# Attention woven between the matmuls of the MLP in one written-out order

## The chip, the cores and the metric

The kernel runs on 1 core of one Trainium2 chip. The core has five engines with queues of their own: PE (TensorE, matmuls; its weight loads are shown as PEld), DVE (VectorE), ACT (ScalarE), POOL (GpSimd) and SP (SyncE, which here only issues DMAs). SBUF is the working memory, PSUM the memory that PE writes its results to. The metric is the device time of one execution in microseconds (us), the median of several runs.

## The reference, cut to what matters

Two stages. The first is a linear attention with a decaying state, for 4 batches, 8 heads, 768 positions and head size 48:

```python
for t in range(S):
    cur = np.einsum('bhd,bhe->bhde', u[None] * kt, vt)
    y[:, :, t] = np.einsum('bhd,bhde->bhe', rt, state + cur)
    state = wt[:, :, :, None] * state + np.einsum('bhd,bhe->bhde', kt, vt)
```

Its output, as 3072 tokens of 8 x 48 = 384 features, goes through an MLP with 2048 hidden features:

```python
h = x @ w_in            # [3072, 384] @ [384, 2048]
r = np.maximum(h, 0.0)
g = s * (r * r) + b
return (g @ w_out).astype(np.float32)   # [3072, 2048] @ [2048, 384]
```

All inputs and the output are fp32.

## The kernel before, in words

Attention works on chunks of 128 positions: 4 batches x 6 chunks = 24 chunks, one batch after the other, each with all 8 heads. Per chunk, four loads (`rt`, `kt`, `vt`, issued by POOL and cast to bf16 on the way, L100 to L106; `wt`, fp32, issued by SP, L109). ACT takes the logarithm of w (`logw`, L114), PE forms its running sums by two triangular matmuls (`cums_i`, `cums_e`, L119, L126) and the sums of a whole chunk by eight one-column matmuls (L131). ACT takes the exponentials (`RA` L141, `KAi` L144, `lam` L153), DVE multiplies r and k by them (`PRD`, L165, L173), PE transposes the products per pair of heads (`trps`, L202), ACT copies them out (`RTKT`, L211), PE forms the scores (`mt_ps`, L217), DVE masks them (`mt_sb`, L227), PE multiplies by v and by the state (`y_ps`, L238, L255). The state goes on by `delta_ps` (L269), an addition on DVE (L291) and a product on POOL (L297); the odd heads' states are moved to partitions 64 to 111 by a DMA on SP (L309). POOL and DVE form the diagonal term (L183, L185, L188, L190), DVE adds it (`x_sb`, L321), PE transposes the result (L330) and ACT copies it to `xT` (L338), which holds the input of the MLP for all 3072 tokens.

The MLP is written behind the attention. The sum of w_out over its rows, times b, comes first (L347 to L360). Then there are six tiles of 512 tokens. For each, 16 groups of 3 matmuls give 128 hidden features by 512 tokens (`h_ps`, L367), ACT takes the relu (`rh`, L375), DVE squares it (`gT`, L376); after those, four groups of 16 matmuls give 128 tokens by 384 features (`o_ps`, L389), DVE scales and adds (`o_sb`, L399), SP stores (L408).

The framework's scheduler sets the order of each engine's instructions, by the order in the text and by when inputs are ready. It also loads ACT's function table anew where logarithm and exponential follow each other (21 + 13 + 6 + 2 loads in the profile).

Of the kernel before, what the change touches and what calls it, by code (L numbers as in the profile page):

```python
# [16 lines left out]
def kernel(  # L18
# [16 lines left out]
    L = 128  # L35
    NCH = S // L
    HD = H * D
    d_model, d_ff = moe_w_in.shape
    n_tok = out.shape[0]
    KT = d_model // 128  # L40
    FT = d_ff // 128
    TOKCH = 512
    NTC = n_tok // TOKCH
# [4 lines left out]
    make_identity(nc, identity)  # L48

    tri_strict = const.tile([128, 128], BF16, name="tri_strict", tag="tri_strict")  # L50
    make_upper_triangular(nc, tri_strict, val=1.0, diag=False)
    tri_incl = const.tile([128, 128], BF16, name="tri_incl", tag="tri_incl")
    make_upper_triangular(nc, tri_incl, val=1.0, diag=True)

    ones_col = const.tile([128, 1], BF16, name="ones_col", tag="ones_col")
    nc.gpsimd.memset(ones_col, 1.0)
    ones_row = const.tile([1, 128], BF16, name="ones_row", tag="ones_row")
    nc.gpsimd.memset(ones_row, 1.0)

    u_bc = const.tile([128, H, D], BF16, name="u_bc", tag="u_bc")  # L60
    nc.gpsimd.dma_start(out=u_bc, in_=u.partition_broadcast(128))

    s_bc = const.tile([128, 1], FP32, name="s_bc", tag="s_bc")
    nc.sync.dma_start(out=s_bc, in_=moe_s.partition_broadcast(128))
    b_sc = const.tile([1, 1], FP32, name="b_sc", tag="b_sc")
    nc.sync.dma_start(out=b_sc, in_=moe_b.partition_broadcast(1))

    w_in_sb = const.tile([128, KT, d_ff], BF16, name="w_in_sb", tag="w_in_sb")
    nc.gpsimd.dma_start(
        out=w_in_sb, in_=moe_w_in.rearrange("(kt p) f -> p kt f", p=128)  # L70
    )
    w_out_sb = const.tile([128, FT, d_model], BF16, name="w_out_sb", tag="w_out_sb")
    nc.gpsimd.dma_start(
        out=w_out_sb, in_=moe_w_out.rearrange("(ft p) n -> p ft n", p=128)
    )

    xT = const.tile([128, KT, n_tok], BF16, name="xT", tag="xT")
    bconst = const.tile([128, d_model], FP32, name="bconst", tag="bconst")

    with (  # L80
        tc.tile_pool(name="ain", bufs=1) as ain,
        tc.tile_pool(name="aprep", bufs=1) as aprep,
        tc.tile_pool(name="atrans", bufs=1) as atrans,
        tc.tile_pool(name="astate", bufs=1) as astate,
        tc.tile_pool(name="apsum", bufs=1, space=bass.MemoryType.PSUM) as apsum,
    ):
        state0 = None
        state_pk = None
        for bb in range(B):
            for cc in range(NCH):  # L90
                t0 = cc * L
                tok0 = bb * S + t0
                is_first = cc == 0
                is_last = cc == NCH - 1

                rt = ain.tile([128, H, D], BF16, name="rt", tag="rt", bufs=3)
                kt_ = ain.tile([128, H, D], BF16, name="kt", tag="kt", bufs=3)
                vt = ain.tile([128, H, D], BF16, name="vt", tag="vt", bufs=3)
# [340 lines left out]
```

## Time and profile before

| what | value |
|---|---|
| median of 3 runs | 344.73 us (343.74 to 346.08) |
| span of the profiled execution, first to last instruction | 342.3 us |
| the profiled execution's own time | not listed; the three runs shown lie 1.4 to 3.8 us above the span |
| PE busy | 235.2 us, 69% of the span |
| DVE, ACT, POOL busy | 186.5, 181.9, 152.7 us |
| DMA | 20.44 MB, 110233 packets, 104578 of them under 512 bytes |

The busy times are sums over the whole span, and the span has two stages with different limits: attention until about 209 us and the MLP behind it. A busy share says little without the stage that it belongs to. In the chain of waits the MLP's two matmul lines hold 18.2% of the span each, and no other line holds over 5%.

### The profile page before, as it was taken

To read this page: it belongs to the slowest core of one execution; us is meant where nothing else is said; L and a number is where in the kernel's file an instruction comes from. 1 tells how busy PE (TensorE), PEld (TensorE's weight loads), DVE (VectorE), ACT (ScalarE), POOL (GpSimd) and SP (SyncE) were. 2 spreads that over 40 slices of the span, in tenths; PEclk is the share of its full clock that TensorE was granted. 3 is DMA by queue.
4 is the path that set the end of the run, shared out by engine and by line. 5 is a ranking of instruction groups with operands and counts; after the bars stand their busy time and mean duration, and the time that the engine had idled before them with its cause. 6 is when DMAs were issued, how large, how long until landed. Compare 5 with 4: busy or idle time off the path is not lost.

```text
span 342.3 us, 5002 instructions
## 1 busy us (share of the span) xinstructions
PE 235.2 (69%) x1865; PEld 142.0 (41%) x1865; DVE 186.5 (54%) x260; ACT 181.9 (53%) x280; POOL 152.7 (45%) x199
## 2 busy tenths in 40 slices
PE   1112646565644567555566747999999999999995
PEld 0001434344432344443445523455554545546453
DVE  0001658775457448675468531855829367393761
ACT  4064665856638966679762420924609155190740
POOL 9102999999998779887793510000000000000000
PEclk9999999999999999999999999999999999999999
DMA  7999899999997978979492400001010110201101
GB/s 113 201 182 131 55 64 68 116 63 75 71 69 61 94 60 65 72 59 82 28 52 13 25 6 0 0 25 69 2 69 24 48 46 2 93 0 48 46 23 69
DMA packets 110233, 20.44 MB, mean 60 GB/s; under 512 B 104578, under 2 KB 109826, under 8 KB 110210
## 3 DMA queue, kind: packets, MB, share of 16 engines
q0 software_dynamic: 77488, 10.33, 45.5%
q1 hardware_dynamic: 32722, 9.81, 13.3%
q8 instruction: 14, 0.23, 0.3%
q14 instruction: 9, 0.07, 0.1%
HBM read 25.36 MB, written 4.72 MB: 88 GB/s over the span
## 4 chain that ended last, share of the span: by engine, by line
PE 46%; ACT 11%; POOL 7%; issue 6%; DVE 5%; DMA 5%; DVEq 0%; POOLq 0%; ACTq 0%
PE o_ps L389 18%; PE h_ps L367 18%; DMA vt<-in_v_dram 5%; ACT L114 3%; DVE mt_sb L227 2%; PE trps L202 2%; ACT RTKT L211 2%; PE mt_ps L217 2%; POOL state L297 2%; ACT logw L114 2%; PE colsum_ps L347 1%; PE y_ps L238 1%; DVE PRD L173 1%; POOL rk L183 1%; POOL rt L100 1%
## 5 line engine op out<-in xcount | busy, mean ns | idle before, releaser
L375 ACT ACTIVATE rh<-h_ps 128x512 bf16<-128x512 f32 x96 | 57.3, 597 | 56.9 <-DVE o_sb L399 52.2
L376 DVE SCALAR_TENSOR_TENSOR gT<-rh 128x512 bf16<-128x512 bf16 x96 | 62.5, 692 | 10.8 <-ACT rh L375 10.8
L389 PE MATMUL o_ps<-w_out_sb,gT 128*128 128x384 bf16 x384 | 63.4, 326 | 0.0
L367 PE MATMUL h_ps<-xT,w_in_sb 128*128 128x512 bf16 x288 | 63.3, 379 | 0.0
L389 PEld LDWEIGHTS <-gT 128*128 128x128 bf16 x384 | 37.6, 98 | 25.5
L367 PEld LDWEIGHTS <-w_in_sb 128*128 128x128 bf16 x288 | 28.0, 98 | 33.5 <-issue 0.5
L126 PE MATMUL cums_e<-logw,tri_strict 128*128 128x384 bf16 x24 | 11.6, 482 | 44.0 <-ACT logw L114 25.8
L202 PE MATMUL trps<-identity,PRD 128*112 128x128 bf16 x192 | 29.1, 312 | 15.5 <-DVE PRD L165 8.8
L399 DVE SCALAR_TENSOR_TENSOR o_sb<-o_ps,s_bc,bconst 128x384 f32<-128x384 f32 x24 | 14.8, 617 | 43.4 <-PE o_ps L389 43.4
L165 DVE SCALAR_TENSOR_TENSOR PRD<-rt,RA 128x384 bf16<-128x384 bf16 x24 | 18.4, 766 | 34.7 <-DMA rt<-in_r_dram 31.8
L183 POOL TENSOR_TENSOR rk<-rt,kt 128x384 bf16<-128x384 bf16 x24 | 24.2, 1007 | 23.0 <-DMA kt<-in_k_dram 22.8
L211 ACT COPY RTKT<-trps 112x1024 bf16<-112x1024 bf16 x24 | 24.1, 1006 | 17.6 <-PE y_ps L255 13.9
L202 PEld LDWEIGHTS <-PRD 128*112 128x112 bf16 x192 | 24.7, 204 | 20.9 <-issue 16.0
L114 ACT ACT_TABLE_LOAD x21 | 26.9, 1283 | 11.5 <-DMA wt<-in_w_dram 9.5
L227 DVE TENSOR_TENSOR mt_sb<-mt_ps,tri_strict 128x1024 bf16<-128x1024 f32 x24 | 29.2, 1215 | 6.5 <-PE mt_ps L217 6.5
L173 DVE SCALAR_TENSOR_TENSOR PRD<-kt,KAi 128x384 bf16<-128x384 bf16 x24 | 30.3, 1261 | 3.1 <-DMA kt<-in_k_dram 2.5
L188 DVE TENSOR_REDUCE cdiag<-rku 128x8 bf16<-128x384 bf16 x24 | 13.2, 549 | 32.6 <-POOL ydiag L190 20.6
L106 POOL DMA_DIRECT2D vt<-in_v_dram x24 | 22.4, 933 | 14.0 <-PE y_ps L255 10.8
L185 POOL TENSOR_TENSOR rku<-rk,u_bc 128x384 bf16<-128x384 bf16 x24 | 24.5, 1022 | 1.1 <-DVE cdiag L188 0.7
L144 ACT ACTIVATE KAi<-cums_i 128x384 bf16<-128x384 f32 x24 | 11.8, 490 | 24.1 <-PE cums_i L131 15.8
L100 POOL DMA_DIRECT2D rt<-in_r_dram x24 | 22.1, 922 | 0.0
L103 POOL DMA_DIRECT2D kt<-in_k_dram x24 | 22.0, 918 | 0.0
(50 smaller groups left out, 280.6 us busy)
## 6 DMA issues: line engine op xcount, KB each, us to landing
wt<-in_w_dram SPq DMA_DIRECT2D x24, 192.0 KB, 3.3
out_dram<-o_sb SPq DMA_DIRECT2D x24, 192.0 KB, 1.9
rt<-in_r_dram POOLq DMA_DIRECT2D x24, 96.0 KB, 3.4
kt<-in_k_dram POOLq DMA_DIRECT2D x24, 96.0 KB, 3.5
vt<-in_v_dram POOLq DMA_DIRECT2D x24, 96.0 KB, 3.3
w_in_sb<-in_moe_w_in_dram POOLq DMA_DIRECT2D x1, 1536.0 KB, 13.9
w_out_sb<-in_moe_w_out_dram POOLq DMA_DIRECT2D x1, 1536.0 KB, 23.8
state_pk<-state SPq DMA_DIRECT2D x20, 18.0 KB, 2.0
```

What stands on the lines that cost most here:

```text
L100: nc.gpsimd.dma_start(out=rt, in_=r[bb, :, t0 : t0 + L, :].transpose([1, 0, 2]))
L114: nc.scalar.activation(out=logw, in_=wt, func=AF.Ln)
L173: nc.vector.scalar_tensor_tensor(out=PRD[:, 1, :, :, 0:48], in0=kt_v, scalar=1.0, in1=KAi_v, op0=ALU.bypass, op1=ALU.mult,)
L183: nc.gpsimd.tensor_tensor(out=rk, in0=rt, in1=kt_, op=ALU.mult)
L185: nc.gpsimd.tensor_tensor(out=rku, in0=rk, in1=u_bc, op=ALU.mult)
L202: nc.tensor.matmul(trps[0:112, slot, :], lhsT=src[:, 0:112], rhs=identity, is_transpose=True, start=(slot == 0), stop=(slot == 7),)
L211: nc.any.tensor_copy(out=RTKT[0:112], in_=trps[0:112])
L227: nc.vector.tensor_tensor(out=mt_sb, in0=mt_ps, in1=tri_strict.unsqueeze(1).to_broadcast([128, H, 128]), op=ALU.mult,)
L367: nc.tensor.matmul(h_ps, lhsT=w_in_sb[:, kt, ft * 128 : (ft + 1) * 128], rhs=xT[:, kt, T * TOKCH : (T + 1) * TOKCH], start=(kt == 0), stop ...
L375: nc.scalar.activation(out=rh, in_=h_ps, func=AF.Relu)
L376: nc.vector.scalar_tensor_tensor(out=gT[:, ft, :], in0=rh, scalar=1.0, in1=rh, op0=ALU.bypass, op1=ALU.mult,)
L389: nc.tensor.matmul(o_ps, lhsT=gT[:, ft, tt * 128 : (tt + 1) * 128], rhs=w_out_sb[:, ft, :], start=(ft == 0), stop=(ft == FT - 1),)
```

## The change

The whole kernel is one written-out order. Every step is a function that issues its instructions, and a list of keys sets when each is called; the framework's scheduler is switched off (`manual_schedule`), so each engine runs its instructions in the order of the keys.

Chunks are numbered with the batch as the fast index (chunk n is position chunk n // 4 of batch n % 4), and an MLP tile is one position chunk of all four batches, 512 tokens. The first four chunks stand 2 keys apart ahead of key 0, all others 4 keys apart from key 0 on. A key holds one group of 3 `h_ps` matmuls (`g1`) with its relu and square, and from tile 1 on one quarter of an `o_ps` group (`g2`, 4 matmuls) of the tile before.

Other edits: all loads are fp32 on SP's queue; the weights come in 8 pieces of 0.8 MB through a staging buffer and POOL casts them (`cast_in`, `cast_out`); POOL also casts v (`vb`). Head pairs are padded from 96 to 128 rows, with zeros set once, so the state of a pair is one block and the DMA of the odd heads falls away; one exponential over 768 columns stands in for two, one product over 768 columns for two; the transposed products are copied out in two halves, on DVE and on ACT; one function table holds logarithm and exponential and is loaded once. The square is a plain `tensor_tensor`. PSUM: one two-bank buffer that `cums` and `mt_ps` share (tag "A"), two banks for `trps`, `d_ps`, `y_ps`, `xt_ps` (tag "B"), three for `h_ps`, one for `o_ps`.

```diff
+    ctx.enter_context(tc.manual_schedule())
+    nc.scalar.preload_act_table_set("natural_log_exp_and_others")
...
+    def load(n):
...
+        for src, dst in ((w, c["w"]), (r, c["rk"][:, 0]), (k, c["rk"][:, 1]), (v, c["v"])):
+            nc.sync.dma_start(out=dst, in_=src[bb, :, t0 : t0 + L, :].transpose([1, 0, 2]))
...
+    def pool1(n):
+        nc.gpsimd.tensor_tensor(out=rkp, in0=..., in1=..., op=ALU.mult)
+        nc.gpsimd.tensor_tensor(out=rku..., in0=rkp, in1=u_bc, op=ALU.mult)
+        nc.gpsimd.tensor_copy(out=vb, in_=c["v"])
...
+    def pool2(n):
+        nc.gpsimd.tensor_tensor(out=yd, in0=c["v"], in1=c["cd"]..., op=ALU.mult)
...
+    def cum(n):
+        ps = psA.tile([128, 2, 512], FP32, name="cums", tag="A")
...
+    def expo(n):
+        nc.scalar.activation(out=E, in_=ps[:, :, 0:HD], func=AF.Exp)
+            nc.scalar.activation(out=lam, in_=ps[:, 0, HD : HD + HP], func=AF.Exp)
...
+    def mult(n):
+        nc.vector.tensor_tensor(out=prd..., in0=c["rk"]..., in1=c["E"]..., op=ALU.mult)
...
+    def tevac(n):
+        nc.vector.tensor_copy(out=RT, in_=c["trps"][:, 0:HP, :])
+        nc.scalar.copy(out=KT_, in_=c["trps"][:, HP : 2 * HP, :])
...
+    def mt(n):
+        ps = psA.tile([128, 2, HP, 128], FP32, name="mt_ps", tag="A")
...
+    def square(T, ft):
+        nc.vector.tensor_tensor(out=gT[T][:, ft, :], in0=rh, in1=rh, op=ALU.mult)
...
+    def base(n):
+        return -24 + 2 * n if n < B else 4 * (n - B)
+    for n in range(N):
+        q = base(n)
+        at(q + 0.00, ln, n)
+        at(q + 0.01, pool1, n)
+        at(q + 1.20, cum, n)
+        at(q + 2.00, expo, n)
+        at(q + 2.01, cdiag, n)
+        at(q + 3.00, mult, n)
+        at(q + 3.01, lam2, n)
+        at(q + 3.02, pool2, n)
+        at(q + 4.20, trans, n)
+        at(q + 5.00, tevac, n)
+        at(q + 6.20, mt, n)
+        at(q + 7.00, mask, n)
+        at(q + 8.10, dmm, n)
+        at(q + 8.30, supd, n)
+        at(q + 8.20, ymm, n)
+        at(q + 9.00, yevac, n)
+        at(q + 10.20, xtr, n)
+        at(q + 11.00, xevac, n)
+    def g1key(T, i):
+        return i if T == 0 else 24 + 16 * (T - 1) + i
+    def g2key(T, i):
+        return 17.5 + 1.4 * i if T == 0 else g1key(T, 15) + 2 + i
+    for T in range(NT):
+        for ft in range(FT):
+            q = g1key(T, ft)
+            at(q + 0.40, g1, T, ft)
+            at(q + 0.45, relu, T, ft)
+            at(q + 1.10, square, T, ft)
...
+    order = [(load, 1), (load_win, 0), (load, 2), (load_win, 1), (load, 3)]
+    order += [(load_win, 2), (load_win, 3), (load_wout, 0), (load_wout, 1)]
+    order += [(load, 4), (load_wout, 2), (load_wout, 3), (load, 5), (load, 6)]
...
+    for i in range(NPIECE):
+        at(-10 + i, cast_in, i)
+        at(1.05 + 3 * i, cast_out, i)
```

Three places in the order. In the rows a number behind a name tells one buffer from another.

PE, a chunk's scores. Before, in the attention stage, all that PE has between two score groups is attention:

```order
L217 MATMUL mt_ps_1120<-RTKT_1118 128x128
...
L202 MATMUL trps_1286<-identity_58,PRD_1274 112x128
...
L119 MATMUL cums_i_1448<-logw_1446,tri_incl_68 128x384
...
L269 MATMUL delta_ps_1317<-vt_1248,PRD_1274 48x48
...
L238 MATMUL y_ps_1131<-vt_1071,mt_sb_1129 128x48
...
L330 MATMUL xt_ps_1165<-identity_58,x_sb_1163 128x128
```

Now, from `cums` of one chunk to `mt_ps` of the chunk before it (`h_ps` and `o_ps` are the MLP's):

```order
L169 MATMUL cums_1648<-logw2_104,tri_strict_86 128x384
...
L413 MATMUL h_ps_1655<-xT_1193,w_in0_94 128x512
...
L446 MATMUL o_ps_1668<-w_out0_98,gT_1125 128x384
...
L364 MATMUL xt_ps_1680<-identity_85,x_sb_1641 128x128
...
L255 MATMUL mt_ps_1684<-RT_1643,KTr_1644 128x128
```

One group of `h_ps`, one of `o_ps` and three transposes stand between the two, and `cums` and `mt_ps` take turns in one PSUM buffer.

ACT at the same place. Before:

```order
L211 COPY RTKT<-trps 112x1024
L144 ACTIVATE KAi<-cums_i 128x384
L114 ACT_TABLE_LOAD
L114 ACTIVATE logw<-wt 128x384
L338 COPY xT<-xt_ps 128x3x128
L141 ACT_TABLE_LOAD
L141 ACTIVATE RA<-cums_e 128x384
```

Now, four keys:

```order
L426 ACTIVATE rh_1639<-h_ps_1635 128x512
L245 COPY KTr_1644<-trps_1621 128x512
L426 ACTIVATE rh_1659<-h_ps_1655 128x512
L191 ACTIVATE E_1673<-cums_1648 128x768
L195 ACTIVATE lam_1675<-cums_1648 128x4
L426 ACTIVATE rh_1697<-h_ps_1693 128x512
L379 COPY xT_1703<-xt_ps_1680 128x3x128
L426 ACTIVATE rh_1717<-h_ps_1713 128x512
L127 ACTIVATE logw0_102<-wt_1286 128x8x48
```

The table loads are gone, four relus stand between the attention's steps, and the exponential `E` of a chunk stands behind a relu whose `h_ps` comes behind that chunk's `cums` on PE.

POOL ahead of the first MLP group. Before, POOL's rows are attention steps and load issues:

```order
L183 TENSOR_TENSOR rk<-rt,kt 128x384
L185 TENSOR_TENSOR rku<-rk,u_bc 128x384
L100 DMA rt<-in_r_dram 128x8x48
L297 TENSOR_TENSOR state_1157<-stmp,lam 48x384
L106 DMA vt<-in_v_dram 128x8x48
L190 TENSOR_TENSOR ydiag<-vt,cdiag 128x384
```

Now, with the last of the first four chunks (`yd_380` is chunk 3's):

```order
L156 TENSOR_TENSOR yd_320<-vt_149,cd_285 128x384
L215 TENSOR_TENSOR l2_378<-lam_331,par_89 128x8
L156 TENSOR_TENSOR yd_380<-vt_158,cd_333 128x384
L528 CAST w_in0_94<-wi_st_145 128x1536
L528 CAST w_in1_95<-wi_st_154 128x1536
L528 CAST w_in2_96<-wi_st_163 128x1536
L528 CAST w_in3_97<-wi_st_165 128x1536
L132 TENSOR_TENSOR rkp_497<-rkt_172 128x384
```

POOL issues no loads any more, and four casts of 1536 columns stand back to back.

## Rows read from the trace of the kernel before

**Rows 1.** The page: length of the span, number of instructions.

```profile
span 342.3 us, 5002 instructions
```

**Rows 2.** Busy time by stretch: PE, PEld, DVE, ACT, POOL, then clock, DMA, GB/s.

```profile
30.00:209.00 179.00, 101.69 (x1146) 72.77 (x1147) 109.06 (x140) 111.53 (x165) 143.01 (x177) 1.00 0.86 60
```

**Rows 3.** Chain of waits in order of time, the end: start us, us, what.

```profile
224.56 10.40 PE o_ps L389 x64
234.96 10.36 PE h_ps L367 x48
...
338.80 0.62 DVE o_sb L399
```

**Rows 4.** Timeline, weight loads of the first MLP matmuls (384 columns): start, length, instruction.

```profile
211.89 0.13 PEld L347 LDWEIGHTS <-ones_col 128*1 128x1 bf16 x1 [0.19 <-issue]
212.21 0.13 PEld L347 LDWEIGHTS <-ones_col 128*1 128x1 bf16 x1 [0.19 <-issue]
```

**Rows 5.** Groups by line and form, ACT: busy us, mean ns | idle us before.

```profile
L375 ACT ACTIVATE rh<-h_ps 128x512 bf16<-128x512 f32 x96 | 57.3, 597 | 56.9 <-DVE o_sb L399 52.2
L144 ACT ACTIVATE KAi<-cums_i 128x384 bf16<-128x384 f32 x24 | 11.8, 490 | 24.1 <-PE cums_i L131 15.8 <-PE cums_i L119 4.1 <-DVE PRD L173 4.1
```

**Rows 6.** The same view, DVE.

```profile
L376 DVE SCALAR_TENSOR_TENSOR gT<-rh 128x512 bf16<-128x512 bf16 x96 | 62.5, 692 | 10.8 <-ACT rh L375 10.8
L173 DVE SCALAR_TENSOR_TENSOR PRD<-kt,KAi 128x384 bf16<-128x384 bf16 x24 | 30.3, 1261 | 3.1 <-DMA kt<-in_k_dram 2.5 <-ACT KAi L144 0.4
L227 DVE TENSOR_TENSOR mt_sb<-mt_ps,tri_strict 128x1024 bf16<-128x1024 f32 x24 | 29.2, 1215 | 6.5 <-PE mt_ps L217 6.5
L165 DVE SCALAR_TENSOR_TENSOR PRD<-rt,RA 128x384 bf16<-128x384 bf16 x24 | 18.4, 766 | 34.7 <-DMA rt<-in_r_dram 31.8 <-PE delta_ps L269 2.8
L399 DVE SCALAR_TENSOR_TENSOR o_sb<-o_ps,s_bc,bconst 128x384 f32<-128x384 f32 x24 | 14.8, 617 | 43.4 <-PE o_ps L389 43.4
L321 DVE TENSOR_TENSOR x_sb<-y_ps,ydiag 128x384 bf16<-128x384 f32 x24 | 13.3, 556 | 14.4 <-PE y_ps L255 13.2 <-PE y_ps L238 1.0
L188 DVE TENSOR_REDUCE cdiag<-rku 128x8 bf16<-128x384 bf16 x24 | 13.2, 549 | 32.6 <-POOL ydiag L190 20.6 <-POOL rku L185 12.0
L291 DVE TENSOR_TENSOR stmp<-delta_ps,state 48x384 bf16<-48x384 f32 x16 | 8.7, 543 | 7.4 <-POOL state L297 6.4 <-PE delta_ps L269 0.9
```

**Rows 7.** Tile rt: duration ns, least/median/most.

```profile
L165 DVE SCALAR_TENSOR_TENSOR PRD<-rt,RA x24: 537/594/1372, 29.8 to 187.4; 128x384 bf16<-128x384 bf16 x24
```

**Rows 8.** Groups by line and form, POOL.

```profile
L297 POOL TENSOR_TENSOR state<-stmp,lam 48x384 bf16<-48x384 bf16 x16 | 13.4, 836 | 5.3 <-issue 3.2 <-PE y_ps L255 1.9
L160 POOL MEMSET PRD<- 128x128 bf16 x24 | 5.1, 214 | 3.2 <-PE delta_ps L269 2.5 <-PE trps L202 0.6
L423 POOL MEMSET const-float32-1.0<- 128x1 f32 x1 | 0.1, 98 | 0.0
```

**Rows 9.** Timeline, DVE, 54 to 59 us.

```profile
54.12 3.53 DVE L173 SCALAR_TENSOR_TENSOR PRD<-kt,KAi 128x384 bf16<-128x384 bf16 x1 [0.95 <-DMA kt<-in_k_dram]
57.57 1.21 DVE L227 TENSOR_TENSOR mt_sb<-mt_ps,tri_strict 128x1024 bf16<-128x1024 f32 x1
```

**Rows 10.** Timeline, POOL, the same stretch.

```profile
54.65 0.93 POOL L183 TENSOR_TENSOR rk<-rt,kt 128x384 bf16<-128x384 bf16 x1
55.53 0.83 POOL L190 TENSOR_TENSOR ydiag<-vt,cdiag 128x384 bf16<-128x384 bf16 x1
56.31 0.91 POOL L185 TENSOR_TENSOR rku<-rk,u_bc 128x384 bf16<-128x384 bf16 x1
```

**Rows 11.** SP's DMA queue, 120 to 200 us: packets, MB, share of 16 engines.

```profile
q1 hardware_dynamic: 7288, 1.17, 8.8%
```

**Rows 12.** The same queue, 215 to 342.3 us (stores of 1536-byte rows).

```profile
q1 hardware_dynamic: 3456, 4.72, 10.4%
```

**Rows 13.** The page: load of w by SP, KB each, us to landing.

```profile
wt<-in_w_dram SPq DMA_DIRECT2D x24, 192.0 KB, 3.3
```

More of the change, by code (lines that the diff above doesn't have):

```diff
@@ new lines @@
+    ones = const.tile([128, 128], BF16, name="ones", tag="ones")
+    par = const.tile([128, 2], FP32, name="par", tag="par")
+    u_bc = const.tile([128, HD], FP32, name="u_bc", tag="u_bc")
+    s_bc = const.tile([128, 1], FP32, name="s_bc", tag="s_bc")
+    b_bc = const.tile([128, 1], FP32, name="b_bc", tag="b_bc")
+    bconst = const.tile([128, d_model], FP32, name="bconst", tag="bconst")
+    w_in_sb = [
+        const.tile([128, KT, PW], BF16, name=f"w_in{i}", tag=f"w_in{i}")
+        for i in range(NPIECE)
+    ]
@@ new lines @@
+    w_out_sb = [
+        const.tile([128, FPP, d_model], BF16, name=f"w_out{i}", tag=f"w_out{i}")
+        for i in range(NPIECE)
+    ]
+    NLW = 3
+    logws = [
+        const.tile([128, H, 64], BF16, name=f"logw{i}", tag=f"logw{i}")
+        for i in range(NLW)
+    ]
+    NPR = 3
+    prds = [
+        const.tile([128, 2, H, 64], BF16, name=f"prd{i}", tag=f"prd{i}")
+        for i in range(NPR)
+    ]
+    cb = [dict() for _ in range(N)]
+    xT = [None] * NT
+    gT = [None] * NT
+    states = [None] * B
@@ new lines, in xtr, with xevac @@
+    def xtr(n):
+        c = cb[n]
+        ps = psB.tile([128, KT, 128], BF16, name="xt_ps", tag="B")
+        for i in range(KT):
+            nc.tensor.matmul(
+                ps[:, i, :],
+                lhsT=c["x"][:, i * 128 : (i + 1) * 128],
+                rhs=identity,
+                is_transpose=True,
+                start=(i == 0),
+                stop=(i == KT - 1),
+            )
+        c["xt_ps"] = ps
+    def xevac(n):
+        c = cb[n]
+        cc, bb = coords(n)
+        if bb == 0:
+            xT[cc] = mlp.tile([128, KT, TOK], BF16, name="xT", tag="xT", bufs=2)
+        nc.scalar.copy(
+            out=xT[cc][:, :, bb * L : (bb + 1) * L], in_=c["xt_ps"]
+        )
@@ new lines, in cast_in, with cast_out @@
+    def cast_in(i):
+        nc.gpsimd.tensor_copy(out=w_in_sb[i], in_=w_in_st[i])
+    def cast_out(i):
+        nc.gpsimd.tensor_copy(out=w_out_sb[i], in_=w_out_st[i])
+    load(0)
+    nc.sync.dma_start(
+        out=u_bc, in_=u.rearrange("h d -> (h d)").partition_broadcast(128)
+    )
+    nc.vector.memset(logws[0], 0.0)
+    make_upper_triangular(nc, tri_strict, val=1.0, diag=False)
+    make_upper_triangular(nc, ntri_incl, val=-1.0, diag=True)
+    make_identity(nc, identity)
+    for i in range(1, NLW):
+        nc.vector.memset(logws[i], 0.0)
@@ L412, with small @@
+    for i in range(NPIECE):
+        at(-10 + i, cast_in, i)
+        at(1.05 + 3 * i, cast_out, i)
+    at(17.3, colsum)
+    def small():
+        nc.sync.dma_start(out=s_bc, in_=moe_s.partition_broadcast(128))
+        nc.sync.dma_start(out=b_bc, in_=moe_b.partition_broadcast(128))
+    at(6.03, small)
+    for n in range(8, N):
+        at(base(n) - 14.5, load, n)
+    ev.sort(key=lambda e: (e[0], e[1]))
+    for _, _, fn, a in ev:
+        fn(*a)
 _INS = ['r', 'k', 'v', 'w', 'u', 'moe_w_in', 'moe_w_out', 'moe_s', 'moe_b']
```

673 lines of the change are left out of this document (340 added, 333 removed).

## The prediction

> **What bounds the kernel now.** I read the page first, then the busy time by stretch, the end of the chain of waits, the groups by line, and at last single stretches of the timeline. The span is 342.3 us [rows 1]. From 30 to 209 us, the attention, PE is busy for 101.7 of 179 us and POOL for 143.0 [rows 2]; no engine is full, and the engines wait for one another along chunk after chunk. Behind that the chain has nothing but matmuls: 64 of `o_ps` in 10.40 us and 48 of `h_ps` in 10.36 us [rows 3], alternating six times, so 124.6 us in which PE is full and the others are not. A group of 4 `o_ps` or 3 `h_ps` matmuls thus takes 0.65 us. The first matmuls behind the attention are started by weight loads 0.32 us apart [rows 4]: 384 columns in 0.32 us are 1.2 GHz, though the granted clock in the rows reads 1.00; the 0.1625 us of `o_ps` are 2.4 GHz. So the attention's matmuls run at the lower level, the MLP's at the upper. The profile's own execution is not listed; I sum against the span and add 344.73 - 342.3 = 2.4 us to stand by the median.
>
> **The change, part by part.** It lays the attention (some 180 us in which PE has room) beside the MLP. The kernel then falls into four pieces.
>
> *Start, until the first `h_ps`: 46 us.* It needs chunks 0 to 3 complete. SP issues 16 loads for them, with two pieces of w_in and `u_bc` between. A load is 1024 packets of 192 bytes; SP's queue moved 7288 small packets in 8.8% of 80 us [rows 11], so 1.0 us a load on 16 engines; at most it is the 3.3 us from issue to landing [rows 13], if they ran one by one. They are queued up to eight deep, so I take 1.0. A 0.79 MB piece is a sixth of the stores' 4.72 MB, which took 10.4% of 127.3 us [rows 12]: 2.2 us. So 1 + 16 x 1.0 + 2 x 2.2 + 0.5, and 2.3 for the last landing: 24 us. Then POOL does four products of 0.84 us [rows 8] and a cast of v, 4 us, and stands before its four weight casts. No row has a cast on POOL. Lower bound: the memset's (214 - 98)/127 = 0.91 ns a column [rows 8], 1.5 us for 1536; upper bound: the two-input product's 836/384 = 2.2 ns [rows 8], 3.3 us. One input lies between, nearer to the memset: I take 2.0, so POOL is through at 36 us.
>
> Chunk 3's product on DVE meets this. In the profile a DVE product that takes 0.537 us alone [rows 7] was asked for at 54.12 us and lasted 3.53 us [rows 9]: POOL's three products ran back to back from 54.65 until 57.22 [rows 10], and DVE came in behind the last. I expect the same behind the four casts: the product ends at 37 us, and transposes, copies, scores, mask (1.2 us [rows 6]), y, addition and copy take 7 to 9 us at the lower clock. First `h_ps` at 46 us, 37 if the casts held nobody up, 56 if they took 3.3 us and the loads half as long again.
>
> *Woven stretch, one chunk in four keys: 19 periods of 8.4 us, 160 us.* PE per period: 4 groups of `h_ps` and 4 of `o_ps`, 5.2 us [rows 3]; attention 101.7/24 = 4.2 us a chunk at 1.2 GHz [rows 2], half of it at 2.4 GHz, 2.1 us. Sum 7.3. Added is a wait: `cums` and `mt_ps` share a PSUM buffer, so a chunk's scores wait for the next chunk's exponential. ACT takes a relu first (0.6 us [rows 5]), which waits for the `h_ps` behind those `cums`, then 768 columns, 0.49 + 384 x (0.597 - 0.490)/128 = 0.81 us [rows 5], and the small exponential, 0.2. PE has one `o_ps` group and three transposes meanwhile, 0.8 us, so about 0.9 us of stall with everything in PE's queue behind it, the MLP too: 8.2 us.
>
> DVE per period: mask 1.2, two additions 1.1, sum for the diagonal 0.55, output 0.62 [rows 6]; the 768-column product, 0.54 + 384 x (0.692 - 0.537)/128 = 1.0 [rows 6, 7]; a copy of 512 columns from PSUM, 0.6 by interpolation from the addition's 384; four squares. The square was 0.692 us [rows 6] as another operation on the same data; that is the upper bound, half of it, at twice the rate, the lower. I take 0.5, since the fixed part stays. Sum 7.1; successive instructions overlap by 0.08 us (57.65 against 57.57 [rows 9]), 12 of them give 1.0 back: 6.1. Added is the waiting for POOL: the 48 products of before took 30.3 + 18.4 us [rows 6] where 48 x 0.537 = 25.8 would do, 0.48 us each; five such operations a period make 2.4 us. DVE is thus at 8.5, PE at 8.2: two engines close to the bound, and I take 8.4. PE alone without a stall gives 7.4; squares at 0.692 give DVE 9.3.
>
> The Trainium skill (SBUF — State Buffer, Who interferes with whom) says that the port pair which DVE and POOL share is an exclusive lock, held for a whole instruction, against DVE operations with two SBUF inputs; the trace agrees with it [rows 9, 10]. By that rule a product that always met a burst of POOL's four operations (some 3 us) would put DVE at 9.1 and the kernel at 273 us, against 260 by the average of the rows.
>
> ACT has 5 us a period, POOL 4 x 0.84 + 0.7 = 4 us (6 with a w_out cast, in chunks 4 to 7): both covered. The 21 + 13 + 6 + 2 table loads become one; ACT is not the bound, so I count nothing for them but what is in the period. The state's DMA is gone and POOL's load issues too; these stood between chunks and are inside the old 7 us a chunk that no longer counts. SP: four loads a period, 4.0 us, and a store of 0.55, covered by 8.4; a store waits at the head of SP's queue for its `o_sb`, but the loads behind it are due 14 keys, some 30 us, later. The 16 `colsum` matmuls fall between tile 0's two halves, where no `h_ps` stands.
>
> *Rest of the MLP: 48 us.* From chunk 23's sums on there are 26 groups of `h_ps` and 43 of `o_ps`, 69 x 0.65 = 45 us, and some 3 us of attention.
>
> *End: 3.5 us*, unchanged: last `o_sb` at 338.80 of 342.3 [rows 1, 3].
>
> Sum: 46 + 160 + 48 + 3.5 = 257.5 us of span, with 2.4 us **260 us**.
>
> **The rivals.**
>
> *DVE and the shared port bound the weave (22%).* For it: 2.4 us of waiting a period is an average over a stage in which POOL partly issued loads; now its operations come in bursts, and squares may stay at 0.692 us. Against: PE is at 8.2 anyway. Period 9.5: 260 + 19 x 1.1 = 281 us. The skill (VectorE: DVE Perf Modes, the perf-mode tier table) gives a plain bf16 `tensor_tensor` in SBUF twice the rate, so some 0.42 us as an estimate; no row here shows one, and with it the sum would be about 6 us lower.
>
> *A late start (10%).* Loads at 1.5 us, casts at 3.3 us, w_out's pieces waiting for staging buffers that only POOL's casts free, with chunk 4's loads queued behind them on SP: 12 us later, 272 us.
>
> *Less contention than I count (16%).* For it: median of the product before is 0.594 us [rows 7], so most meet nothing. Start at 37 us, period 7.6: 260 - 9 - 15 = 236 us.
>
> *The clock falls back in the weave (6%), the other side.* The attention kept PE at the lower level for 180 us at 57% busy [rows 2, 4]; the weave's stalls could do so as well. Then a period is 8 x 1.28 + 4.2 = 14.4 us and more, the 69 groups behind it 88 us: 260 + 19 x 6 + 44, about 420 us. It decides at half: each period at 1.2 GHz costs 6 us, so some 14 of 19 of them (84 us) bring it to 344. Against: with MLP groups in every key PE is over 85% busy, and at the lower level it would be full, which is what raised it at 212 us.
>
> **How the numbers follow.** The forecast has 46%, its own range 246 to 274 (period 7.9 to 9.0, start 42 to 52). The range, 238 to 290, takes in the late start and most of the DVE case; out are the clock's case (6%) and some of the ends of the others, below 20% in all. A change under 1% can't be told from none here. Faster 93%, within 1% 1%, slower 6%: only the clock's case comes near 344.7.
>
> **What would show it.** Right: first `h_ps` at about 46 us with a DVE product of several us beside POOL's casts; `cums` of successive chunks 8.4 us apart; waits of PE at `mt_ps` for `E` or `lam` of about 0.9 us; DVE over 90% busy in the weave, squares near 0.5 us; `o_ps` at 0.1625 us from tile 1 on. Wrong: periods of 9.5 us with squares of 0.7 to 2 us (DVE), a first `h_ps` past 55 us (start), or matmuls of 0.32 us for 384 columns in the weave (clock).

## The result, and the profile after

The changed kernel takes 282.09 us (median of 4 runs, 281.12 to 284.52) against 344.37 us before (343.74 to 346.08): ratio 0.820, 95% interval 0.816 to 0.824. The prediction was 260 us with a range of 238 to 290: the direction and the range hold, and the time lies 22 us above the number, outside the forecast's own range of 246 to 274.

The page of the changed kernel has 62 us less span than [rows 1]. Its first part, and the granted clock in 40 slices of 7 us:

```profile
span 280.3 us, 4354 instructions
PE 192.6 (69%) x1602; PEld 116.6 (42%) x1624; DVE 169.2 (60%) x270; ACT 109.4 (39%) x214; POOL 123.4 (44%) x150
PEclk9999999959879999999999999999999999999999
```

Busy time by stretch (columns as in [rows 2]; the first is one period of the weave, from E to E, the second the MLP's rest):

```profile
179.00:189.40 10.40, 7.38 (x68) 4.58 (x69) 7.24 (x11) 4.44 (x11) 5.02 (x6) 1.00 0.48 95
226.40:276.40 50.00, 48.07 (x300) 26.31 (x303) 21.73 (x43) 17.95 (x32) 0.71 (x1) 1.00 0.11 40
```

In the weave PE is busy for 7.38 of 10.4 us and DVE for 7.24: as in [rows 2] no engine is full. In the rest PE is, as it was in [rows 3]. What PE waits for, over the whole span (us in total, times, longest us):

```profile
PE trps L228 <- DVE stmp L349: 28.1, 16, 4.3
PE mt_ps L255 <- ACT lam L195: 18.6, 16, 1.5
PE cums L169 <- ACT logw L127: 17.4, 5, 5.0
PE mt_ps L255 <- ACT E L191: 6.1, 4, 1.5
```

The third row is, but for 0.3 us, the start, before there is an MLP to weave with. The other three are the weave: 24.7 us at `mt_ps`, which the prediction had, and 28.1 us at `trps`, which it had not. One period on the timeline, one of six alike from chunk 14 to chunk 20 (the rows of its cycle; start us, us, engine, line, operation, idle before):

```profile
178.98 0.82 ACT L191 ACTIVATE E<-cums 128x768 bf16<-128x768 f32 x1
179.67 0.19 ACT L195 ACTIVATE lam<-cums 128x4 f32<-128x4 f32 x1
179.91 0.40 PE L255 MATMUL mt_ps<-RT,KTr 48*128 48x128 bf16 x8 [1.50 <-ACT lam L195]
...
180.35 1.22 DVE L267 TENSOR_TENSOR mt_sb<-mt_ps,tri_strict 128x1024 bf16<-128x1024 f32 x1 [0.80 <-PE mt_ps L255]
...
181.49 1.22 DVE L201 TENSOR_TENSOR prd<-rkt,E 128x768 bf16<-128x768 f32 x1
...
182.63 1.86 DVE L431 TENSOR_TENSOR gT<-rh 128x512 bf16<-128x512 bf16 x2
...
184.41 0.54 DVE L349 TENSOR_TENSOR stmp<-d_ps,st 128x384 bf16<-128x384 f32 x1
185.01 0.61 PE L228 MATMUL trps<-identity,prd 128*128 128x128 bf16 x8 [1.45 <-DVE stmp L349]
...
186.95 0.62 DVE L456 SCALAR_TENSOR_TENSOR o_sb<-o_ps,s_bc,bconst 128x384 f32<-128x384 f32 x1 [2.00 <-PE o_ps L446]
...
187.95 0.41 DVE L244 COPY RT<-trps 128x512 bf16<-128x512 bf16 x1
...
188.40 0.59 ACT L245 COPY KTr<-trps 128x512 bf16<-128x512 bf16 x1 [1.50 <-DVE RT L244]
...
188.88 0.60 ACT L426 ACTIVATE rh<-h_ps 128x512 bf16<-128x512 f32 x1
...
189.37 0.82 ACT L191 ACTIVATE E<-cums 128x768 bf16<-128x768 f32 x1
```

Read it as a ring. `trps` reads `prd`, ready at 182.7, yet it starts at 185.0: `d_ps`, `y_ps`, `trps` and `xt_ps` take turns in the two PSUM banks of tag B, and the bank that `trps` gets is the one of `d_ps`, free only when `stmp` has read it. `stmp` could have run from 183.2 on, when `d_ps` is complete, but two squares stand ahead of it in DVE's queue. Behind `trps` PE does its MLP groups, DVE waits for their `o_ps`, then comes to `RT`, ACT copies `KTr` behind `RT`, then a relu, then E and `lam`, and only those let `mt_ps` have tag A. 7.38 us of PE's work and waits of 1.50 and 1.45 us make 10.33 of the 10.4 us. From chunk 20 on, which has no `d_ps`, the periods are 9.6, 8.5 and 8.5 us.

The groups on DVE that answer to [rows 6], in the weave from 100 to 180 us (busy us, mean ns, idle before):

```profile
L431 DVE TENSOR_TENSOR gT<-rh 128x512 bf16<-128x512 bf16 x33 | 21.6, 667 | 7.7 <-ACT rh L426 7.7
L201 DVE TENSOR_TENSOR prd<-rkt,E 128x768 bf16<-128x768 f32 x8 | 9.9, 1234 | 0.0
L267 DVE TENSOR_TENSOR mt_sb<-mt_ps,tri_strict 128x1024 bf16<-128x1024 f32 x8 | 9.8, 1224 | 5.6 <-PE mt_ps L255 5.6
```

At the start, POOL's casts of w_in (least, median and most ns) and chunk 3's product on DVE, the places of [rows 9, 10]:

```profile
L528 POOL CAST w_in<-wi_st x4: 1462/1465/2200, 29.3 to 34.2; 128x1536 bf16<-128x1536 f32 x4
```
```profile
29.88 1.67 DVE L201 TENSOR_TENSOR prd<-rkt,E 128x768 bf16<-128x768 f32 x1
```

The casts stand at 29.28 to 35.71 us. The first ends at 30.74 and the product at 31.55, so the product came in behind the first; it is the second cast, begun at 30.68, that took the 2200 ns.

### The profile page after: what moved, and what is told of

The parts are those of the page before. It is cut to its first block, busy times and chain, and to the rows that moved or that the text cites. A ratio compares the mean times of both kernels' runs of the same rounds, so it can differ in the third digit from the quotient of the medians.

```text
span 280.3 us, 4354 instructions
## 1 busy us (share of the span) xinstructions
PE 192.6 (69%) x1602; PEld 116.6 (42%) x1624; DVE 169.2 (60%) x270; ACT 109.4 (39%) x214; POOL 123.4 (44%) x150
## 4 chain that ended last, share of the span: by engine, by line
PE 35%; DVE 24%; issue 12%; SPq 9%; ACT 9%; DMA 5%; POOL 3%; DVEq 0%; ACTq 0%; POOLq 0%
PE o_ps L446 11%; PE h_ps L413 11%; SPq L120 8%; DVE prd L201 7%; DVE gT L431 6%; DMA rkt<-in_k_dram 5%; PE trps L228 4%; ACT E L191 4%; DVE o_sb L456 4%; PE o_psh L446 4%; ACT rh L426 4%; DVE stmp L349 3%; PE mt_ps L255 3%; DVE x_sb L322 2%; DVE mt_sb L267 2%
## 5 line engine op out<-in xcount | busy, mean ns | idle before, releaser
L413 PE MATMUL h_ps<-xT,w_in 128*128 128x512 bf16 x266 | 76.4, 394 | 1.9 <-ACT xT L379 0.6
L431 DVE TENSOR_TENSOR gT<-rh 128x512 bf16<-128x512 bf16 x96 | 57.7, 613 | 32.4 <-ACT rh L426 32.3
L446 PE MATMUL o_ps<-w_out,gT 128*128 128x384 bf16 x320 | 64.9, 326 | 1.8 <-DVE o_sb L456 0.7
L228 PE MATMUL trps<-identity,prd 128*128 128x128 bf16 x192 | 17.5, 244 | 30.6 <-DVE stmp L349 28.1
L413 PEld LDWEIGHTS <-w_in 128*128 128x128 bf16 x288 | 25.7, 100 | 21.9 <-issue 3.6
L132 POOL TENSOR_TENSOR rkp<-rkt 128x384 f32<-128x384 f32 x24 | 25.2, 1049 | 18.4 <-DMA rkt<-in_k_dram 18.4
L139 POOL TENSOR_TENSOR rku<-rkp,u_bc 128x384 f32<-128x384 f32 x24 | 31.7, 1320 | 2.9 <-DMA u_bc<-in_u_dram 1.1
L201 DVE TENSOR_TENSOR prd<-rkt,E 128x768 bf16<-128x768 f32 x24 | 29.4, 1227 | 0.3 <-ACT E L191 0.3
L255 PE MATMUL mt_ps<-RT,KTr 48*128 48x128 bf16 x192 | 10.4, 231 | 25.2 <-ACT lam L195 18.6
L156 POOL TENSOR_TENSOR yd<-vt,cd 128x384 bf16<-128x384 f32 x24 | 20.2, 841 | 15.5 <-DVE cd L150 15.4
L191 ACT ACTIVATE E<-cums 128x768 bf16<-128x768 f32 x24 | 19.4, 810 | 3.1 <-PE cums L177 3.0
L352 POOL TENSOR_TENSOR st<-stmp,l 128x384 bf16<-128x384 bf16 x16 | 13.3, 828 | 11.9 <-DVE stmp L349 11.9
```

The costliest lines, as they stand in the source:

```text
L132: nc.gpsimd.tensor_tensor(out=rkp, in0=c["rk"][:, 0].rearrange("t h d -> t (h d)"), in1=c["rk"][:, 1].rearrange("t h d -> t (h d)"), op=AL ...
L139: nc.gpsimd.tensor_tensor(out=rku.rearrange("t h d -> t (h d)"), in0=rkp, in1=u_bc, op=ALU.mult)
L191: nc.scalar.activation(out=E, in_=ps[:, :, 0:HD], func=AF.Exp)
L201: nc.vector.tensor_tensor(out=prd[:, :, :, 0:D].rearrange("t x h d -> t (x h) d"), in0=c["rk"].rearrange("t x h d -> t (x h) d"), in1=c["E ...
L228: nc.tensor.matmul(ps[:, x * HP + p, :], lhsT=c["prd"][:, x, 2 * p : 2 * p + 2, :].rearrange("t h d -> t (h d)"), rhs=identity, is_transpo ...
L255: nc.tensor.matmul(ps[:, sg, p, :], lhsT=c["KT"][pr, p, :], rhs=c["RT"][pr, p, :], start=(p == 0), stop=(p == HP - 1),)
```

## The experiments

Theory 1: PE waits for PSUM banks, `trps` for that of `d_ps` and `mt_ps` for that of `cums`; DVE's order decides how long. Theory 2, the prediction's rival: DVE and the port it shares with POOL hold the period. All edits are to the changed kernel. Before was 343.9 to 344.1 us beside experiments 1 to 10 and 344.3 us beside 11 and 12.

| run | edit | us | ratio to before, interval |
|---|---|---|---|
| the change | | 282.1 | 0.820 (0.816 to 0.824) |
| 1 | third bank for tag B | 256.4 | 0.745 (0.742 to 0.748) |
| 2 | one h_ps buffer fewer | 282.8 | 0.823 (0.818 to 0.828) |
| 3 | all relus later | 286.4 | 0.832 (0.831 to 0.834) |
| 4 | squares later | 272.3 | 0.791 (0.789 to 0.794) |
| 5 | POOL's term out | 268.6 | 0.780 (0.777 to 0.782) |
| 6 | E, lam ahead of KTr | 273.8 | 0.795 (0.791 to 0.799) |
| 7 | 1 and 6 | 246.8 | 0.717 (0.714 to 0.719) |
| 8 | 7, loads reordered | 243.2 | 0.706 (0.704 to 0.708) |
| 9 | 8, one square in four moved | 235.8 | 0.686 (0.683 to 0.688) |
| 10 | 8, POOL's term out | 233.0 | 0.677 (0.674 to 0.679) |
| 11 | 1 and 5 | 252.6 | 0.734 (0.731 to 0.736) |
| 12 | d_ps and stmp earlier | 255.9 | 0.743 (0.741 to 0.746) |

**1 and 2: the bank.**

```diff
-        tc.tile_pool(name="psB", bufs=2, space=bass.MemoryType.PSUM)
+        tc.tile_pool(name="psB", bufs=3, space=bass.MemoryType.PSUM)
-        tc.tile_pool(name="psH", bufs=3, space=bass.MemoryType.PSUM)
+        tc.tile_pool(name="psH", bufs=2, space=bass.MemoryType.PSUM)
```

Experiment 2 has the second pair of lines alone.

> Tag B gets a third PSUM bank, taken from the h_ps buffers (three to two). Theory 1 (the PE waits on a shared PSUM bank): the wait of trps for stmp, 28.1 us in all, falls under 3 us; a steady period goes from 10.4 us to about 9.0 us (10.4 less the 1.45 us of that wait), and with some 16 such periods the time goes from 282 us to about 260 us. Theory 2 (DVE and POOL in each other's way at their shared port set the period): DVE's work in a period is the same, so the period stays at 10.4 us and the time at 282 us within 1%. Either way the PE may wait a little more at h_ps, which has one buffer fewer; the run beside this one shows that alone.

> Two h_ps buffers instead of three, nothing given to tag B: the price of the first experiment's edit alone. Both theories: the wait of trps for stmp stays near 1.45 us a period, and the time is 282 us to 288 us; a h_ps buffer is free again when its relu of 0.5 us is done, and two h_ps groups stand 2 us apart.

The bank brings 25.7 us and the lost buffer alone costs nothing that shows. From the timeline of experiment 1, a steady period:

```profile
158.99 0.40 PE L255 MATMUL mt_ps<-RT,KTr 48*128 48x128 bf16 x8 [1.50 <-ACT lam L195]
...
161.69 1.86 DVE L431 TENSOR_TENSOR gT<-rh 128x512 bf16<-128x512 bf16 x2
...
162.47 0.61 PE L228 MATMUL trps<-identity,prd 128*128 128x128 bf16 x8
...
163.48 0.54 DVE L349 TENSOR_TENSOR stmp<-d_ps,st 128x384 bf16<-128x384 f32 x1
```

DVE does what it did, the squares take the same 1.86 us, but `trps` now stands a microsecond ahead of `stmp` and waits for nothing. Steady periods are 8.8 us, and all 19 go from 182.7 us to 159.3. Theory 2 expected no change.

**12 and 4: the order in place of the bank.**

```diff
-        at(q + 8.10, dmm, n)
-        at(q + 8.30, supd, n)
+        at(q + 6.10, dmm, n)
+        at(q + 6.95, supd, n)
-            st = states[bb]
+            st = c.get("st0", states[bb])
+        c["st0"] = states[bb]
```

The last three lines keep for `ymm` the state that `supd` is about to replace. The edit does two things at once. `stmp` runs earlier, and the tiles of tag B are asked for in another order: `d_ps`, `y_ps`, `trps`, `xt_ps` before, `d_ps`, `xt_ps`, `y_ps`, `trps` now. With two banks that take turns, `trps` then gets the bank of `xt_ps` and no longer that of `d_ps`, which goes to `y_ps`.

> The changed kernel with its two banks of tag B and its three of h_ps, but d_ps and stmp two steps earlier in the order, so that stmp stands ahead of the mask, the product and the squares in VectorE's queue (y_ps still reads the state of before). Theory 1: the bank is free long before trps wants it, the wait of 1.45 us a period goes without another bank, and the time is 252 us to 260 us, as in the first experiment. Theory 2: VectorE does the same work at the same port; the time stays within 1% of 282 us. If only a third bank can take the wait away, because y_ps or xt_ps now wait in its place, 270 us to 282 us.

```diff
-            at(q + 1.10, square, T, ft)
+            at(q + 1.35, square, T, ft)
```

> The square is written a quarter of a step later, so that stmp stands ahead of one of the two squares that ran before it. DVE's work is the same, only its order differs. Theory 1: stmp ends 0.4 us to 0.9 us earlier, the wait of trps for it goes from 1.45 us to 0.6 us to 1.0 us, and the time to 268 us to 275 us. Theory 2: the same work at the same port, so the period stays at 10.4 us and the time within 1% of 282 us.

Experiment 12 takes the same wait away with two banks, and the time is the same within 0.2% of experiment 1. `stmp` runs at 140.02 us in time in which DVE had waited for the scores, `y_ps`, which now gets the bank that `stmp` reads, finds it free, and `trps` has no wait. The wait at `mt_ps` is shorter too, 0.94 us for 1.50. From its timeline:

```profile
140.02 0.55 DVE L350 TENSOR_TENSOR stmp<-d_ps,st 128x384 bf16<-128x384 f32 x1
...
140.46 0.40 PE L255 MATMUL mt_ps<-RT,KTr 48*128 48x128 bf16 x8 [0.94 <-ACT lam L195]
...
143.16 2.36 DVE L432 TENSOR_TENSOR gT<-rh 128x512 bf16<-128x512 bf16 x2
...
143.40 0.33 PE L283 MATMUL y_ps<-st,RT 128*128 128x96 bf16 x4
...
143.78 0.61 PE L228 MATMUL trps<-identity,prd 128*128 128x128 bf16 x8
```

So 12 shows that order alone can do what a bank does, but not how much of it is the earlier `stmp` and how much the other pairing of tiles and banks. Experiment 4 leaves the pairing as it is and puts `stmp` ahead of one square only. It lands where theory 1 put it, with a wait of 0.81 us for 1.45 and steady periods of 9.7 us:

```profile
168.35 0.61 PE L228 MATMUL trps<-identity,prd 128*128 128x128 bf16 x8 [0.81 <-DVE stmp L349]
```

**5 and 11: the port, with and without the bank.**

```diff
-        at(q + 2.01, cdiag, n)
+        if n < 2 * B:
+            at(q + 2.01, cdiag, n)
-        at(q + 3.02, pool2, n)
+        if n < 2 * B:
+            at(q + 3.02, pool2, n)
...
+        if n >= 2 * B:
+            nc.vector.tensor_copy(out=x, in_=c["y_ps"][:, 0:HD])
+            c["x"] = x
+            return
```

The two products `rkp` and `rku` in `pool1` stand behind the same condition.

> From chunk 8 on POOL's diagonal term (rkp, rku, yd) and its sum on DVE are left out, and x_sb is a plain copy of y_ps: the output of these chunks lacks the diagonal term. POOL then works 1.8 us of a period instead of 5.2 us, and DVE has little to wait for at the port. Theory 2: DVE sets the period, so that what the port costs it and the 0.55 us of cd come off it: 10.4 us goes to about 8.5 us over 12 to 16 periods, the time to 250 us to 258 us, and the PE waits next to nothing for stmp. Theory 1: the period is the chain of E, mt_ps, mask, product, squares, stmp, trps; shorter squares and products (0.62 us to 0.45 us, 1.23 us to 0.95 us) bring stmp 0.5 us to 0.9 us forward and no more; the trps wait goes from 1.45 us to 0.6 us to 0.9 us, that of mt_ps stays 1.5 us, and the time is 268 us to 275 us.

> The first experiment (a third bank for tag B) with POOL's diagonal term and its sum left out from chunk 8 on, as in the fifth (the output of these chunks lacks that term). Theory 1: with the bank given, the product and the squares are no longer between the PE and its next matmul; the period is the PE's 7.3 us and the 1.5 us at mt_ps, which the port does not touch, and the time stays within 1% of the first experiment's 256 us. Theory 2: the port's share comes off here as it did in the fifth, 13 us, and the time is about 243 us.

DVE's groups of experiment 5, 100 to 180 us, answer to those of the change:

```profile
L440 DVE TENSOR_TENSOR gT<-rh 128x512 bf16<-128x512 bf16 x36 | 15.2, 422 | 13.1 <-ACT rh L435 13.1
L272 DVE TENSOR_TENSOR mt_sb<-mt_ps,tri_strict 128x1024 bf16<-128x1024 f32 x9 | 11.0, 1225 | 6.7 <-PE mt_ps L260 6.7
L206 DVE TENSOR_TENSOR prd<-rkt,E 128x768 bf16<-128x768 f32 x9 | 8.5, 948 | 0.0
```

So POOL's work beside them costs a square 0.25 us on average (667 against 422 ns) and the product 0.29 us (1234 against 948); the mask, which reads PSUM, is as long as before (1224 and 1225 ns). Per period that is 4 x 0.25 + 0.29 = 1.3 us. Taking it away is worth 13.5 us while tag B has two banks, and 3.8 us (1.5%) with three; both edits also take the 0.55 us of `cd` off DVE, so the port's share is at most that. Most of the gain with two banks is the wait at `trps`, which goes from 28.1 to 16.6 us in all; in a steady period of experiment 5:

```profile
164.28 0.61 PE L233 MATMUL trps<-identity,prd 128*128 128x128 bf16 x8 [0.48 <-DVE stmp L358]
```

So the port was part of the loss, but through the bank: it makes the queue ahead of `stmp` longer. With the bank given, the steady periods of experiments 1 and 11 are the same 8.8 us, with POOL's term and without. My bound of 1% for experiment 11 was missed, and theory 2's 243 us by far more. Of the difference 3.0 us lie between the E of chunks 8 and 15; 1.7 us of them are one period of 10.5 us in the profile of experiment 1, in which the granted clock was 0.50 for 3.4 us, and why the others are shorter was not settled.

**3 and 6: the wait at mt_ps.**

```diff
-            at(q + 0.45, relu, T, ft)
+            at(q + 1.05, relu, T, ft)
```

> The relu behind cums is written after E and lam, so that ScalarE takes the two exponentials first. Theory 1: the wait of mt_ps for lam, 18.6 us in all and 1.50 us in a steady period, falls under 0.5 us a period; E starts about 1 us earlier after cums, the period goes from 10.4 us to about 9.2 us, the time to about 264 us. Theory 2: E comes earlier but the period is held by DVE; the time stays within 1% of 282 us.

```diff
-        at(q + 1.20, cum, n)
-        at(q + 2.00, expo, n)
+        at(q + 0.80, cum, n)
+        at(q + 0.95, expo, n)
```

> The sums and E, lam are given earlier places in the order, so that ScalarE takes E and lam ahead of KTr and of the relu behind it, while the relus keep their places (in the third experiment all relus moved too, and the squares behind them). The PE's order is the same in the woven part. Theory 1: mt_ps then waits for KTr alone, its wait goes from 1.50 us to 0.2 us to 0.5 us, and if the wait for stmp stays at 1.45 us the period is 9.2 us and the time 258 us to 265 us; if the chain through mask, product and stmp gives part of it back, 270 us. Theory 2: DVE has the same work, period 10.4 us, time within 1% of 282 us.

Experiment 3 missed on both theories: it is 4.3 us slower than the change. From its timeline:

```profile
166.59 0.58 ACT L245 COPY KTr<-trps 128x512 bf16<-128x512 bf16 x1 [5.84 <-DVE RT L244]
...
167.07 0.60 ACT L426 ACTIVATE rh<-h_ps 128x512 bf16<-128x512 f32 x1
167.56 0.82 ACT L191 ACTIVATE E<-cums 128x768 bf16<-128x768 f32 x1
...
168.50 0.40 PE L255 MATMUL mt_ps<-RT,KTr 48*128 48x128 bf16 x8 [1.55 <-ACT lam L195]
...
168.97 0.82 DVE L431 TENSOR_TENSOR gT<-rh 128x512 bf16<-128x512 bf16 x1 [0.37 <-ACT rh L426]
...
169.72 1.21 DVE L267 TENSOR_TENSOR mt_sb<-mt_ps,tri_strict 128x1024 bf16<-128x1024 f32 x1
```

One relu went behind E, but the edit moved every relu, and the one of the step before came to stand between `KTr` and E: the wait is 1.55 us, as it was. And the square of a relu that is now late stands ahead of the mask, which starts 0.8 us behind the end of `mt_ps` and takes product, squares and `stmp` with it.

Experiment 6 does what 3 was meant to do: E runs while ACT would have waited for `RT`. From its timeline:

```profile
161.07 0.40 PE L255 MATMUL mt_ps<-RT,KTr 48*128 48x128 bf16 x8 [0.24 <-ACT KTr L245]
...
163.44 1.69 DVE L201 TENSOR_TENSOR prd<-rkt,E 128x768 bf16<-128x768 f32 x1
...
166.62 0.61 PE L228 MATMUL trps<-identity,prd 128*128 128x128 bf16 x8 [1.91 <-DVE stmp L349]
```

Of the 1.50 us at `mt_ps` 1.26 are gone, but the wait at `trps` rose from 1.45 to 1.91 us: the product comes at another moment of POOL's burst and takes 1.69 us in place of 1.22. The steady period is 9.6 us, and the gain 8 us, not the 20 that the wait alone would give: 273.8 us lies outside both theories.

**7 to 10: what comes next.**

> The first and the sixth experiment together: a third bank for tag B, and E and lam ahead of KTr. Theory 1: both waits are gone, the PE is the bound in the woven part with 7.3 us of work a period and some 0.3 us of waits; 8.8 us of the first experiment goes to 7.6 us over 17 periods, and its 256 us to about 236 us. Theory 2: DVE needs 6.8 us and more of a period; its queue becomes the bound near 8.5 us, and the time stays above 250 us.

Experiment 8 adds to the edits of the seventh:

```diff
-    order += [(load_win, 2), (load_win, 3), (load_wout, 0), (load_wout, 1)]
-    order += [(load, 4), (load_wout, 2), (load_wout, 3), (load, 5), (load, 6)]
-    order += [(load, 7)]
+    order += [(load_win, 2), (load_win, 3), (load, 4), (load, 5)]
+    order += [(load_wout, 0), (load, 6), (load_wout, 1), (load, 7)]
+    order += [(load_wout, 2), (load_wout, 3)]
-        at(1.05 + 3 * i, cast_out, i)
+        at(4.05 + 3 * i, cast_out, i)
```

> The seventh kernel, with the loads of chunks 4 and 5 ahead of all of w_out and those of 6 and 7 between its pieces, and the casts of w_out three steps later in POOL's order. Both theories: chunk 4's E starts some 4 us to 6 us earlier than in the seventh (42 us in the first experiment), and the gap of 11 us between the E of chunks 5 and 6 closes to about 8 us; 5 us to 9 us off the time, unless the casts of w_out now come late for colsum and the first o_ps, which would give it back.

And experiment 9 to those of the eighth:

```diff
-            at(q + 1.10, square, T, ft)
+            at(q + (2.02 if ft % 4 == 1 else 1.10), square, T, ft)
```

> The eighth kernel with one square in four, the one that stands ahead of the mask in VectorE's order, put behind the product; VectorE's work is the same. Theory 1: mask and product come 0.4 us to 0.8 us earlier, the PE's wait of 0.48 us for the product at trps goes, and the period goes from 8.15 us to 7.7 us: 243 us to about 235 us. Theory 2, now that the two waits on banks are out: VectorE is busy over 7.5 us of the 8.15 us, so its queue is the bound and the order within it moves nothing; the time stays within 1.5% of 243 us.

> The eighth kernel with POOL's diagonal term and its sum left out from chunk 8 on, as in the fifth experiment (the output of these chunks lacks that term). Theory 2, as the next bound of this kernel: the product takes 0.95 us in place of 1.66 us, squares 0.42 us in place of 0.61 us, cd's 0.55 us goes; the waits of trps for the product disappear and the period falls to the PE's own 7.4 us: 243 us to about 232 us. Theory 1 without the port: the period is held by PE, KTr and the banks, and the time stays within 1% of 243 us.

Experiment 7 has no wait on a bank left in its steady periods, but these are 8.15 us and not 7.6, and its time lies between the two theories: the product, still 1.69 us long behind a square and the mask, is now what `trps` waits for. From its timeline:

```profile
145.22 1.69 DVE L201 TENSOR_TENSOR prd<-rkt,E 128x768 bf16<-128x768 f32 x1
...
146.96 0.62 PE L228 MATMUL trps<-identity,prd 128*128 128x128 bf16 x8 [0.47 <-DVE prd L201]
```

The loads of experiment 8 bring 3.6 us, less than expected: the gap from chunk 5's E to chunk 6's goes from 11.4 to 7.1 us, but chunk 4's E comes only 0.5 us earlier (40.5 us). In experiment 7 that gap also holds a stretch of 6.8 us at a granted clock of 0.50, which experiment 8 doesn't have, so the loads' own share isn't separated. In experiments 9 and 10 each theory misses one: order alone gives 7.4 us with all of POOL's work in place, and taking POOL's term away gives 10.1 us. Both end at periods of 7.5 us. The new order also moves the product away from POOL's burst: between 100 and 180 us it takes 1.26 us on average in experiment 9, for 1.66 in experiment 7. One of experiment 9, by stretch (columns as in [rows 2]):

```profile
142.00:149.50 7.50, 7.27 (x70) 4.42 (x69) 7.13 (x12) 4.53 (x9) 5.29 (x7) 1.00 0.68 131
```

PE is busy for 7.27 of 7.50 us: here PE bounds the weave, with DVE right behind. Experiment 9 computes all of the reference, and at 235.8 us it is the fastest such kernel, 46 us below the change.

## Why the prediction was right, and where it was not

*The ground of the gain: right.* PE had room in the attention, and the MLP beside it took it: PE's work per period is 7.38 us (forecast 7.3), and a group of four `o_ps` in the chain of the weave takes 0.66 us, as in [rows 3], which is 2.4 GHz. No run separates the weave from what was changed with it (the 42 table loads of 1.28 us each, the state's DMA, POOL's load issues, the joined exponential and product), so how much of the 62 us is the weave's alone stays open.

*The wait at `mt_ps`: seen, too small.* Forecast 0.9 us, measured 1.50. The prediction put one relu ahead of E; in the trace `KTr`, which waits for `RT`, stands ahead of that relu, and `RT` behind DVE's output and addition.

*The period of 8.4 us: this step failed.* The prediction followed the sharing of tag A and wrote "PE has one `o_ps` group and three transposes meanwhile", then took PE's 8.2 us as free of further waits. It never counted the tiles of tag B against its two banks. With the wait of 1.45 us at `trps`, and 0.6 us more than forecast at `mt_ps`, a steady period is 10.4 us; over all 19 it is 9.6 us and 182.7 us in place of 160. With a third bank the 19 periods take 159.3 us (experiment 1), and with two banks and another order of `d_ps` and `stmp` the kernel takes 255.9 (experiment 12). So the wait at `trps` is the miss.

*DVE at 8.5 us a period: too much.* It is busy for 7.24. The square at 0.5 us was between 0.42 alone and 0.67 in company. The Trainium skill (VectorE: DVE Perf Modes, the perf-mode tier table) led to an estimate of 0.42 us, and experiment 5 agrees with 0.422. The port was counted at 2.4 us and costs 1.3; the copy `RT` was counted at 0.6 us and takes 0.41. The sign "DVE over 90% busy" was wrong: 70%. The rival of less contention argued with a median of 0.594 us [rows 7], which is that of the r products alone. The k products of the kernel before have one of 1.079:

```profile
L173 DVE SCALAR_TENSOR_TENSOR PRD<-kt,KAi x24: 537/1079/3528, 32.0 to 192.8; 128x384 bf16<-128x384 bf16 x24
```

*The rival at 281 us: right number, wrong ground.* It wanted periods of 9.5 us from DVE and the port. DVE's busy time in a steady period was about the same in experiment 1 (7.22 us) and more in 12 (7.72), and the time fell by 26 us. That 282.1 us lies within the stated range, which was drawn to take in most of this rival, is thus luck: the wait that made the time was not in the sum. With two banks the port only lengthens the wait for the bank, and with three it costs a steady period nothing (experiments 1 and 11). In experiments 7 and 8, with the wait at `mt_ps` cut too, it has a hand in the period, together with the order: `trps` waits for the lengthened product, and either taking POOL's term away (10) or moving a square (9) gives the same 7.5 us.

*The start: 39.75 us for 46.* A cast of 1536 columns takes 1.46 us, which is the lower bound of the prediction and not its 2.0, and the product of chunk 3 lost 0.7 us (1.67 against 0.95 alone) and not the length of four casts. Chunk 4's E, at which the periods begin, is at 43.7 us, so this gave back only 2 to 3 us. The late start's ground, loads queued behind w_out's pieces, did come, one chunk later: the chain goes through chunk 5's k, issued at 41.52 us and landed at 48.69, and chunk 6's E stands 14.2 us behind chunk 5's. The rest took 50.0 us for 48, the end 3.9 for 3.5.

*The clock's rival: it came, small.* The granted clock in the profile fell to 0.50 (1.2 GHz) three times in tile 0. The first time (columns as in [rows 2]), and the stretch ahead of it:

```profile
44.80:55.04 10.24, 5.52 (x52) 2.84 (x51) 6.79 (x9) 5.38 (x11) 7.91 (x9) 1.00 1.29 190
55.04:61.87 6.83, 3.00 (x18) 1.90 (x19) 4.71 (x7) 0.68 (x2) 5.83 (x6) 0.50 1.01 180
```

Ahead of it PE was busy for 5.52 of 10.24 us. The three stretches are 13.6 us long, with 8.7 us of matmuls in them; at 2.4 GHz these would take half, so at most 4.4 us were lost. From 82.3 us to the end the clock is 1.00, with PE busy for 71% of a steady period where the prediction counted on over 85%. In experiment 8 PE is busy for 13.3 of the 20 us from 44 to 64 us (in the change for 10.2), and its slices show no fall:

```profile
PEclk9999999999999999999999999999999999999998
```

## What to carry to other kernels

When an order is woven by hand, write down for each PSUM tag which tile gets the bank of which, and who must have read that one; a reader that held PE up for 5.8 us in all of the chunk-by-chunk kernel (`stmp`) holds up the whole weave when its place in DVE's queue is behind work that isn't urgent. Such a wait can be cured by order as well as by another bank: 255.9 us with an earlier reader and another pairing of tiles and banks, 256.4 with the bank, and 272.3 with the reader one square earlier and nothing else. Take one wait of a ring away, and look at once for the next: of experiment 6's 1.26 us a period more than a third came back at `trps`.

## What was not expected of the hardware

POOL's products lengthen DVE's operations that have all operands in SBUF, and by how much depends on the moment: a square takes 0.41 to 1.63 us, the 768-column product 0.95 to 2.01 us, while the mask from PSUM stays at 1.22 us with POOL's term and without. DVE need not wait for a whole run of POOL's instructions, as [rows 9, 10] had suggested: the product got in after the first of four casts that stood back to back, and the second cast took 2.20 us where the others took 1.46. [rows 10] also leave out what POOL did when that product of before was asked for, at 54.12 us: it issued a load, which the changed kernel's POOL never does.

```profile
53.76 0.88 POOL L100 DMA_DIRECT2D rt<-in_r_dram  x1
```

Whether that is why DVE waited there through all three products, no run shows. The Trainium skill (SBUF — State Buffer, Who interferes with whom) says that a DVE instruction with two SBUF inputs meets POOL's reads, and one with at most one SBUF input does not, outside DVE's 2-port modes; the trace agrees: the mask has one of its inputs in SBUF and stays at 1.22 us, the square has both there and goes from 0.42 to 0.67 us on average.
